# Attention and an ELU layer on one core: a path with constant scales, P V on array quarters, shared row sums, weight steps one by one

## The chip, the cores and the metric

The kernel runs on one core of a Trainium2 chip. The metric is the device time of one execution in microseconds (us). The kernel before took 647.91 us (median of 3 runs, 647.34 to 647.96). One more execution was run under the profiler; all rows below come from it. Of the core's engines, PE (TensorE) multiplies matrices, ACT (ScalarE) evaluates functions, DVE (VectorE) and POOL (GpSimd) work elementwise, and SP issues the DMAs.

## The reference

Attention over 48 heads (4 batches of 12 heads, 448 tokens, 64 columns a head), with scores bounded by a cap, and then two matrix products with an ELU between them. The cap is 30.

```
scale = 1.0 / np.sqrt(q.shape[-1])
scores = scale * np.matmul(q, k.transpose(0, 1, 3, 2))
scores = cap * np.tanh(scores / cap)
scores = scores - np.max(scores, axis=-1, keepdims=True)
attn = np.exp(scores)
attn = attn / (np.sum(attn, axis=-1, keepdims=True) + 1e-09)
attn_out = np.matmul(attn, v).astype(np.float32)
x = attn_out.transpose(0, 2, 1, 3).reshape(B * S, H * D)       # 1792 x 768
h = x @ w_in                                                    # 768 x 2048
g = np.where(h > 0.0, h, np.exp(np.minimum(h, 0.0)) - 1.0)
out = (g @ w_out).astype(np.float32)                            # 2048 x 768
```

## The kernel before

**Attention.** Two heads form a pair (24 pairs), and two pairs a round (12 rounds, `n`). Scores are kept with the keys on the partitions. The 448 keys of a head are cut into 64 + 3 x 128 (`NT` = 4 key tiles). A round has seven groups of scores: group 0 holds the first 64 keys of all four heads, stacked in one tile of two PSUM banks (`tile0`, plain f32); groups 1 to 3 and 4 to 6 hold the 128-key tiles of pair 0 and of pair 1 (`scores`, three products of f32 split in a high and a low part, `qkh` and `qkl`, which `prep_qk` makes on DVE). For each group ACT runs a tanh in place in PSUM and an exp into the SBUF tile `p` (`act`); the scale of each is a [128,1] tile that was worked out from the cap (`tsc`, `cap`).

**P V and row sums.** `values(n, i, t)` multiplies key tile `t` of pair `i` into the bank `pv` (tag `pv0`, one for both pairs of a round, one after the other): two matmuls, a head in each half of the array's columns. For `t` = 0 all 128 rows are used, with `v` zero in the rows of the other pair. `add` sums the three 128-key tiles of `p` in `u` on DVE, and `sums(n, i)` makes the row sums of a pair in the bank of tag `pv1`: ones times `u`, and a half-ones column times group 0, in four separate 32-row strips. `take` copies `pv` to `num` and the four strips to `sums` on DVE, and four small DMAs fold each pair's sums to 64 partitions; `invert` adds the two parts and eps, takes the reciprocal and sends it to DRAM; `spread` reads it back on all partitions, and `normalise` multiplies.

**PSUM.** The eight banks are three score tiles of two banks (tag `s`) and one bank each of `pv0` and `pv1`. A score group waits until the exp of the group three before it has read its tile.

**Order.** The order in the attention is written out by hand: `run` collects (time, function) events, sorts them and emits them; the times in `AT` are in units of one score group. Each engine runs its instructions in this order. Beside the attention DVE splits the tokens (`high`, `low`: xh, xl) and prepares the first four weights (`Weights.steps`, five steps a weight: three DVE operations; wq; DVE and POOL; wh; wl).

**The two products** (`Moe`). The tokens are cut in four blocks `t` of 512, 512, 512 and 256, the 2048 hidden columns in 8 rounds `r` of 256. A unit (r, t) has `first` (w_in, two tiles of 128 hidden columns into `pv0` and `pv1`, then `elu` over ACT, DVE, ACT, DVE) and `second` (w_out, six output tiles in three PSUM tiles of tag `s`, with e = 0, 2, 4). For r = 0 ACT copies the result to `acc`, later DVE adds it. PE's order is first(unit i), second(unit i-1). Around each `second` the weight steps of the next round are run: `n // 2` ahead of it and the rest behind it, `n` by block from `WRUN` = (6, 6, 4, 4). Here wq and wh are on ACT, and POOL's addition lies between them.

Which path runs is decided on the chip: every engine loads a flag (`|cap| <= 32`) and branches, to this path or to a general one.

Of the kernel before, what the change touches and what calls it, by code (L numbers as in the profile page):

```python
# [17 lines left out]
P = 128  # L18
# [13 lines left out]
FAST_CAP = 32.0  # L32
TINY = 2.0**-15
# [134 lines left out]
class Tokens:  # L168
# [17 lines left out]
    def high(self, p, t, vector=False):  # L186
# [12 lines left out]
        if vector:  # L199
            self.nc.vector.tensor_copy(out=out, in_=x)  # L200
        else:
            self.nc.scalar.activation(out=out, in_=x, func=AF.Copy)
# [11 lines left out]
class Moe:  # L214
# [57 lines left out]
    def second(self, r, t):  # L272
# [3 lines left out]
        for e in range(0, NC, 2):  # L276
# [46 lines left out]
class Attention:  # L323
# [51 lines left out]
    def tile0(self, n):  # L375
# [33 lines left out]

    def values(self, n, i, t):  # L410

        v = self.v[2 * n + i]
        if t == 0:
            x = [self.p[n, 0][:, j] for j in range(2)]
            self.pv[n, i] = self.ps.tile([P, BANK], F32, name=f"pv{n}_{i}", tag="pv0", bufs=1)
        else:
            pt = self.p[n, GROUP[i, t]]
            x = [pt[:, j] for j in range(2)]
        w = [v[:, t, j * D : j * D + D] for j in range(2)]
        self.two(self.pv[n, i], w, x, start=t == 0, stop=t == NT - 1)  # L420
# [11 lines left out]
    def sums(self, n, i):  # L432

        t = self.sum[n, i] = self.ps.tile([P, BANK], F32, name=f"sum{n}_{i}", tag="pv1", bufs=1)
        u = self.u.pop((n, i))
        work = [(self.ones, u[:, j]) for j in range(2)]
        work += [(self.half[:, i ^ j], self.p[n, 0][:, j]) for j in range(2)]
        for k, (w, x) in enumerate(work):
            self.nc.tensor.matmul(t[k * 32 : k * 32 + 32, :S], w, x, start=True, stop=True)  # L439

    def take(self, n, i, step):
        nc, sb, p = self.nc, self.sb, 2 * n + i
        if step == 0:
            t = self.num[p] = sb.tile([P, S], F32, name=f"num{p}", tag="num", bufs=5)
            nc.vector.tensor_copy(out=t, in_=self.pv.pop((n, i))[:, :S])  # L445
            return
        t = self.early.tile([P, S], F32, name=f"sums{p}", tag="ev", bufs=2)
        nc.vector.tensor_copy(out=t, in_=self.sum.pop((n, i))[:, :S])
        if i == 0:
            self.den[n] = sb.tile([CP, 2, 2, 2 * CN], F32, name=f"den{n}", tag="den", bufs=2)  # L450
        for k in range(4):
            j = slice(k % 2 * CN, k % 2 * CN + CN)
            nc.sync.dma_start(out=self.den[n][:, k // 2, i, j], in_=t[k * 32 : k * 32 + 1, :])

    def invert(self, n):

        nc = self.nc
        t = self.den.pop(n)
        den = t[:, 0]
# [5 lines left out]
        nc.sync.dma_start(  # L465
            out=d.rearrange("j (a n) -> a j n", a=CP), in_=den.rearrange("a i (j n) -> a (i j) n", j=2)
        )
# [14 lines left out]
    def run(self, weights, moe, raw, rawv):  # L482
# [14 lines left out]
        for n in range(rounds):  # L497
# [6 lines left out]
            for i in range(2):  # L504
                p = 2 * n + i
                for t in range(NT):
                    at(g + AT["values"][i][t], self.values, n, i, t)
                for step in range(2):
                    at(g + AT["add"][i][step], self.add, n, i, step)
                    at(g + AT["prep"][i][step], self.prep_qk, p + 2, step)  # L510
                    at(g + AT["take"][i][step], self.take, n, i, step)
                at(g + AT["sums"][i], self.sums, n, i)
# [3 lines left out]
                at(g + AT["load_v"][i], self.load_v, p + 2)  # L516
            at(min(g + AT["invert"], end + END["invert"]), self.invert, n)
# [3 lines left out]
            for k in range(2):  # L521
# [3 lines left out]
                for p in ([c] if 0 <= c < PPB else []) + [PPB + i for i in range(PPB) if n == 8 + i // 2]:  # L525
                    at(g + AT["split"][k], *((self.x.high, p, 0, True) if k == 0 else (self.x.low, p, 0)))
# [26 lines left out]
def general_attention(nc, sb, ps, x, con, src):  # L553
# [5 lines left out]
    for p in range(NPAIR):  # L559
# [3 lines left out]
        for j in range(2):  # L563
            o, o0 = slice(j * D, j * D + D), slice((p % 2 ^ j) * D, (p % 2 ^ j) * D + D)
# [34 lines left out]
def constants(nc, pool, cap):  # L599
# [3 lines left out]
    flag = pool.tile([1, 1], I32, name="flag")  # L603
# [4 lines left out]
    nc.vector.tensor_single_scalar(out=flag, in_=con.eps[0:1, :], scalar=FAST_CAP, op=ALU.is_le)  # L608
# [7 lines left out]
def attention_elu_kernel(tc, qk, v, cap, w, out):  # L616
    nc = tc.nc
    src = (qk, v)
    with ExitStack() as outer:
# [14 lines left out]
        fast = nc.values_load(flag[0:1, 0:1], min_val=0, max_val=1)  # L634

        def path(general):
            tag = "gf"[not general]
# [28 lines left out]
        with tc.If(fast > 0) as branch:  # L666
# [48 lines left out]
```

## Time and profile before

| | |
|---|---|
| median of 3 runs | 647.91 us |
| profiled execution | 648.52 us |
| its span | 646.7 us |
| PE busy | 629.4 us, 97% |
| DVE busy | 463.8 us, 72% |
| ACT busy | 296.7 us, 46% |
| POOL busy | 61.2 us, 9% |

The span is what the profile covers; 1.8 us of the execution lie around it. The attention fills the first 172 us, the rest is the two products. A share over the whole span says little here, since the stages have different limits; the rows below are therefore from short stretches. A granted clock (PEclk) of 1.00 is TensorE's higher level of 2.4 GHz.

### The profile page before, as it was taken

What the parts mean: (1) busy time and instruction counts of PE and PEld (TensorE: products, weight loads), DVE (VectorE), ACT (ScalarE), POOL (GpSimd) and SP (SyncE); (2) the same over time, 40 slices, a digit from 0 to 9 for tenths busy, and PEclk for the clock granted to TensorE, in tenths of its full rate; (3) what the DMA queues carried; (4) which work ended last, traced back from release to release, by engine and by line L of the source; (5) the groups of instructions that cost most, each with busy time, mean ns of one, the idle gap of its engine ahead of it and who ended that gap; (6) DMA issues with size and microseconds to landing.
All of it is one profiled execution on the core that took longest, in us unless ns stands there. A gap on an engine that the chain in (4) does not pass through costs nothing.

```text
span 646.7 us, 8796 instructions
## 1 busy us (share of the span) xinstructions
PE 629.4 (97%) x3408; PEld 463.0 (72%) x3408; DVE 463.8 (72%) x696; ACT 296.7 (46%) x396; POOL 61.2 (9%) x40
## 2 busy tenths in 40 slices
PE   5999999999999899999999999999999999999997
PEld 3334444334478788888888888888888888888886
DVE  4789999999667744776767577666857766776454
ACT  6999999999916544222231322223132322222110
POOL 0010100101001111121111111011111111211000
PEclk9999999999999999999999999999999999999999
DMA  4445565544123111121111111121111111200224
GB/s 162 140 141 186 158 185 148 168 125 132 32 77 126 51 49 50 49 98 31 68 50 50 49 50 55 43 76 71 50 50 50 50 50 49 70 30 0 98 97 152
DMA packets 30065, 54.38 MB, mean 84 GB/s; under 512 B 13377, under 2 KB 17473, under 8 KB 30017
## 3 DMA queue, kind: packets, MB, share of 16 engines
q1 hardware_dynamic: 30016, 53.75, 25.7%
q8 instruction: 29, 0.48, 0.3%
q14 instruction: 20, 0.16, 0.1%
HBM read 47.97 MB, written 5.59 MB: 83 GB/s over the span
## 4 chain that ended last, share of the span: by engine, by line
PE 78%; DVE 13%; DMA 3%; ACT 2%; issue 2%; POOL 1%; SPq 1%; DVEq 0%; POOLq 0%; ACTq 0%
PE o L226 11%; PE o L227 11%; PE o L228 11%; PE h L226 11%; PE h L227 11%; PE h L228 11%; PE pv L408 6%; PE s L366 4%; DVE u L430 3%; DVE xl L211 2%; PE sum L439 2%; DVE qkl L361 1%; DVE num L445 1%; PE s L383 1%; DMA den<-sums 1%
## 5 line engine op out<-in xcount | busy, mean ns | idle before, releaser
L226 PE MATMUL o<-gh,wh 128*128 128x512 f32 (+1 forms) x380 | 138.8, 365 | 2.7 <-ACT acc L285 2.7
L227 PE MATMUL o<-gl,wh 128*128 128x512 f32 (+1 forms) x380 | 138.9, 365 | 0.0
L228 PE MATMUL o<-gh,wl 128*128 128x512 f32 (+1 forms) x380 | 138.7, 365 | 0.0
L227 PE MATMUL h<-xl,wh 128*128 128x512 f32 x288 | 112.2, 390 | 0.3 <-DVE xl L211 0.3
L226 PE MATMUL h<-xh,wh 128*128 128x512 f32 x288 | 112.4, 390 | 0.0
L228 PE MATMUL h<-xh,wl 128*128 128x512 f32 x288 | 112.1, 389 | 0.0
L300 DVE TENSOR_TENSOR acc<-o,acc 128x1024 f32<-128x1024 f32 (+1 forms) x83 | 88.6, 1091 | 31.8 <-PE o L228 31.8
L240 ACT ACTIVATE e<-h 128x512 f32<-128x512 f32 (+1 forms) x64 | 34.7, 542 | 138.8 <-PE h L228 138.8
L401 ACT ACTIVATE p<-s,cap 128x896 f32<-128x896 f32 x84 | 84.7, 1008 | 2.7
L399 ACT ACTIVATE s<-s,tsc 128x896 f32<-128x896 f32 x84 | 81.9, 975 | 5.3 <-PE s L383 2.8
L226 PEld LDWEIGHTS o<-gh,wh 128*128 128x128 f32 x380 | 72.1, 190 | 14.5 <-ACT acc L285 2.9
L408 PE MATMUL pv<-p,vf 128*64 128x448 f32 x368 | 79.3, 552 | 3.0 <-DVE num L445 3.0
L228 PEld LDWEIGHTS o<-gh,wl 128*128 128x128 f32 x380 | 72.1, 190 | 11.4
L227 PEld LDWEIGHTS o<-gl,wh 128*128 128x128 f32 x380 | 72.0, 190 | 11.4
L249 ACT ACTIVATE gh<-e 128x512 fp32r<-128x512 f32 (+1 forms) x64 | 37.0, 578 | 90.2 <-DVE e L244 90.2
L250 DVE TENSOR_TENSOR gl<-e,gh 128x512 fp32r<-128x512 f32 (+1 forms) x64 | 40.0, 626 | 41.2 <-ACT gh L249 41.2
L142 POOL TENSOR_TENSOR pre<-pre,wq 128x768 int32<-128x768 int32 x18 | 34.7, 1929 | 339.7 <-DVE pre L139 339.7
L241 DVE TENSOR_SCALAR e<-e 128x512 f32<-128x512 f32 (+1 forms) x64 | 25.0, 391 | 56.5 <-ACT e L240 56.5
L226 PEld LDWEIGHTS h<-xh,wh 128*128 128x128 f32 x288 | 54.1, 188 | 12.4 <-DVE e L244 0.7
L227 PEld LDWEIGHTS h<-xl,wh 128*128 128x128 f32 x288 | 54.1, 188 | 11.6 <-DVE xl L211 0.7
L228 PEld LDWEIGHTS h<-xh,wl 128*128 128x128 f32 x288 | 54.1, 188 | 11.3
L408 PEld LDWEIGHTS pv<-p,vf 128*64 128x64 f32 x368 | 22.3, 136 | 44.1 <-issue 31.6
(78 smaller groups left out, 770.6 us busy)
## 6 DMA issues: line engine op xcount, KB each, us to landing
pre<-in_w_dram SPq DMA_DIRECT2D x18, 768.0 KB, 4.2
wr<-in_w_dram SPq DMA_DIRECT2D x14, 768.0 KB, 4.2
raw<-in_qk_dram SPq DMA_DIRECT2D x22, 448.0 KB, 4.5
vf<-in_v_dram SPq DMA_DIRECT2D x23, 256.0 KB, 4.1
rb<-rec SPq DMA_DIRECT2D x48, 112.0 KB, 2.9
out_dram<-acc SPq DMA_DIRECT2D x9, 512.0 KB, 2.7
den<-sums SPq DMA_DIRECT2D x96, 1.8 KB, 2.3
pre<-in_qk_dram SPq DMA_DIRECT2D x2, 256.0 KB, 4.1
```

The lines of the kernel that those rows point to most:

```text
L142: nc.gpsimd.tensor_tensor(out=vi, in0=vi, in1=q, op=ALU.add)
L226: mm(acc, wh[:, m, :], ph, start=first, stop=False)
L227: mm(acc, wh[:, m, :], pl, start=False, stop=False)
L228: mm(acc, wl[:, m, :], ph, start=False, stop=last)
L240: nc.scalar.activation(out=ev, in_=h, func=AF.Exp)
L249: nc.scalar.activation(out=gh, in_=ev, func=AF.Copy)
L250: nc.vector.tensor_tensor(out=gl, in0=ev, in1=gh.bitcast(F32), op=ALU.subtract)
L300: self.nc.vector.tensor_tensor(out=o, in0=s, in1=o, op=ALU.add)
L366: yield lambda a=a, b=b, i=i: self.nc.tensor.matmul(s, a[o, k], b[o, :S], start=i == 0, stop=i == 2)
L399: self.nc.scalar.activation(out=s, in_=s, func=AF.Tanh, scale=self.con.tsc[:, 0:1])
L401: self.nc.scalar.activation(out=pt, in_=s, func=AF.Exp, scale=self.con.cap[:, 0:1])
L408: self.nc.tensor.matmul(out[o, :S], w[j], x[j], **flags)
```

## The change

Six things change together.

- A third path, taken first when the cap is exactly 30: tanh and exp have their scales as constants in the instruction. A second flag is computed and loaded for it. The path otherwise equals the fast one.
- Group 0 is stacked by pair in all partitions (pair `i` in half `i`), and its P V uses quarters of the array: `values0` runs four matmuls of 64 rows x 64 columns, into two banks, one a pair. So `pv` has tag `pv0` for pair 0 and `pv1` for pair 1, and `sums` comes into `pv0` after pair 0's `num` has been taken.
- The row sums of both pairs are made in one bank, accumulated over `u` and group 0. One DVE instruction takes them and adds eps; four DMAs a round instead of eight; `invert` is a reciprocal alone.
- The high part of the tokens of block 0 (`high`) is made by ACT and no longer by DVE.
- The times in `AT` follow: both first tiles at 2.7, one `sums` at 8.25 and one `take_sums` at 8.9.
- `WRUN` gives the steps of a unit one place each: ahead of `second`, and behind each of its three output groups.

```
-WRUN = (6, 6, 4, 4)
+WRUN = ((2, 2, 1, 1), (2, 2, 1, 1), (2, 1, 1, 1), (1, 1, 1, 1))
 AT = {
-    "values": ((2.7, 2.8, 3.1, 4.7), (6.4, 6.5, 7.75, 7.8)),
+    "values0": 2.7, "values": ((2.8, 3.1, 4.7), (6.4, 6.5, 7.75)),
-    "sums": (6.2, 8.5), "take": ((5.35, 6.7), (8.75, 9.86)),
+    "sums": 8.25, "take": (5.35, 8.05), "take_sums": 8.9,
...
+            self.wt.run(steps[e // 2])            # in second, behind each e
...
-            n = WRUN[units[i - 1][1]]
-            self.wt.run(n // 2)
-            self.second(*units[i - 1])
-            self.wt.run(n - n // 2)
+            steps = WRUN[units[i - 1][1]]
+            self.wt.run(steps[0])
+            self.second(*units[i - 1], steps[1:])
...
-                o, at = slice(j * D, j * D + D), (i ^ j) * D            # tile0
+                o, at = slice(j * D, j * D + D), i * D
...
-        self.nc.scalar.activation(out=s, in_=s, func=AF.Tanh, scale=self.con.tsc[:, 0:1])
+        self.nc.scalar.activation(out=s, in_=s, func=AF.Tanh, scale=self.con.tanh_scale)
...
-        self.nc.scalar.activation(out=pt, in_=s, func=AF.Exp, scale=self.con.cap[:, 0:1])
+        self.nc.scalar.activation(out=pt, in_=s, func=AF.Exp, scale=self.con.exp_scale)
...
+    def values0(self, n):
+        for i in range(2):
+            o = slice(i * D, i * D + D)
+            pv = self.ps.tile([P, BANK], F32, name=f"pv{n}_{i}", tag=f"pv{i}", bufs=1)
+            self.pv[n, i] = pv
+            v = self.v[2 * n + i]
+            for j in range(2):
+                c = slice(j * D, j * D + D)
+                self.nc.tensor.matmul(
+                    pv[c, :S], v[o, 0, c], self.p[n, 0][o, j], start=True, stop=False
+                )
...
+    def sums(self, n):
+        t = self.sum[n] = self.ps.tile([P, BANK], F32, name=f"sum{n}", tag="pv0", bufs=1)
+        u = [self.u.pop((n, i)) for i in range(2)]
+        for last in range(2):
+            for k in range(4):
+                i, j = divmod(k, 2)
+                w, x = (self.half[:, i], self.p[n, 0][:, j]) if last else (self.ones, u[i][:, j])
+                self.nc.tensor.matmul(
+                    t[k * 32 : k * 32 + 32, :S], w, x, start=not last, stop=bool(last)
+                )
...
+    def take_sums(self, n):
+        nc, sb = self.nc, self.sb
+        t = self.early.tile([P, BANK], F32, name=f"sums{n}", tag="ev", bufs=2)[:, :S]
+        nc.vector.tensor_scalar_add(t, self.sum.pop(n)[:, :S], self.con.eps[:, 0:1])
+        self.den[n] = sb.tile([CP, 4, CN], F32, name=f"den{n}", tag="den", bufs=2)
+        for k in range(4):
+            nc.sync.dma_start(out=self.den[n][:, k, :], in_=t[k * 32 : k * 32 + 1, :])
...
-        nc.vector.scalar_tensor_tensor(
-            out=den, in0=den, scalar=self.con.eps[:CP, 0:1], in1=t[:, 1], op0=ALU.add, op1=ALU.add
-        )
...
+    nc.vector.tensor_single_scalar(out=flag[:, 1:2], in_=con.cap[0:1, :], scalar=USUAL_CAP, op=ALU.is_equal)
...
-        fast = nc.values_load(flag[0:1, 0:1], min_val=0, max_val=1)
+        fast, usual = (nc.values_load(flag[0:1, k : k + 1], min_val=0, max_val=1) for k in range(2))
+            if tag == "u":
+                con.tanh_scale, con.exp_scale = D**-0.5 / USUAL_CAP, USUAL_CAP
```

**PE, one round.** In a row's name the first number is the group, or the pair in `pv` and `sum`; the last is a running number of the buffer. Before, from the last product of pair 0 to pair 1's row sums (the six rows of the two score groups between are left out):

```order
L408 MATMUL pv_0_177<-p_3_183,pre 64x448 x2
L383 MATMUL s_0_217<-raw_126 64x448 x2
L383 MATMUL s_0_217<-raw_152 64x448 x2
L439 MATMUL sum_0_235<-u_0_185,ones 32x448 x2
L439 MATMUL sum_0_235<-p_0_147,half 32x448 x2
L408 MATMUL pv_1_240<-p_0_147,vf_115 64x448 x2
L408 MATMUL pv_1_240<-p_4_193,vf_115 64x448 x2
...
L408 MATMUL pv_1_240<-p_5_214,vf_115 64x448 x2
L408 MATMUL pv_1_240<-p_6_231,vf_115 64x448 x2
L439 MATMUL sum_1_277<-u_1_233,ones 32x448 x2
L439 MATMUL sum_1_277<-p_0_147,half 32x448 x2
```

And now, from `values0` on (score groups left out):

```order
L417 MATMUL pv_0_192<-p_0_162,pre 64x448 x2
L417 MATMUL pv_1_195<-p_0_162,vf_130 64x448 x2
L406 MATMUL pv_0_192<-p_1_165,pre 64x448 x2
...
L406 MATMUL pv_0_192<-p_3_201,pre 64x448 x2
L381 MATMUL s_0_235<-raw_141 64x448 x2
L381 MATMUL s_0_235<-raw_167 64x448 x2
L406 MATMUL pv_1_195<-p_4_211,vf_130 64x448 x2
L406 MATMUL pv_1_195<-p_5_232,vf_130 64x448 x2
...
L406 MATMUL pv_1_195<-p_6_249,vf_130 64x448 x2
L446 MATMUL sum_282<-u_0_203,ones 32x448 x2
L446 MATMUL sum_282<-u_1_251,ones 32x448 x2
L446 MATMUL sum_282<-p_0_162,half 32x448 x4
```

Pair 1's product with group 0 has moved from its own place behind `tile0` to pair 0's, and pair 0's row sums have moved behind pair 1's last product.

**ACT, the copies of unit (0, 1).** Before, from the end of the ELU of unit (0, 2):

```order
L249 ACTIVATE gh_2_2298<-e_2_2294 128x512
L135 ACTIVATE wq_2225<-wr_2076 128x768
L149 ACTIVATE wh_2305<-wv_2224 128x768
L285 ACTIVATE acc_0_2321<-o_1_0_2308 128x1024
L285 ACTIVATE acc_2_2336<-o_1_2_2323 128x1024
L285 ACTIVATE acc_4_2351<-o_1_4_2338 128x1024
```

And now:

```order
L247 ACTIVATE gh_2_2217<-e_2_2213 128x512
L136 ACTIVATE wq_2144<-wr_1995 128x768
L283 ACTIVATE acc_0_2237<-o_1_0_2224 128x1024
L150 ACTIVATE wh_2239<-wv_2143 128x768
L283 ACTIVATE acc_2_2256<-o_1_2_2243 128x1024
L283 ACTIVATE acc_4_2275<-o_1_4_2262 128x1024
```

The weight's high part, which waits for POOL, now stands behind the first copy and ahead of the other two.

**DVE, the additions of unit (6, 1).** Before:

```order
L139 SCALAR_TENSOR_TENSOR wv_4867<-wr_4758,wv_4867 128x768
L300 TENSOR_TENSOR acc_0_2321<-o_1_0_4933,acc_0_2321 128x1024
L300 TENSOR_TENSOR acc_2_2336<-o_1_2_4947,acc_2_2336 128x1024
L300 TENSOR_TENSOR acc_4_2351<-o_1_4_4961,acc_4_2351 128x1024
L153 TENSOR_TENSOR wl_4931<-wv_4867,wh_4930 128x768
```

And now:

```order
L140 SCALAR_TENSOR_TENSOR pre<-pre 128x768
L299 TENSOR_TENSOR acc_0_2237<-o_1_0_4865,acc_0_2237 128x1024
L154 TENSOR_TENSOR wl_4863<-pre,wh_4862 128x768
L124 SCALAR_TENSOR_TENSOR wv_4880<-wr_4804 128x768
L125 TENSOR_SCALAR wv_4880<-wv_4880 128x768
L126 TENSOR_SCALAR wv_4880<-wv_4880 128x768
L299 TENSOR_TENSOR acc_2_2256<-o_1_2_4885,acc_2_2256 128x1024
L299 TENSOR_TENSOR acc_4_2275<-o_1_4_4900,acc_4_2275 128x1024
```

Four weight operations have moved between the additions. The steps of a round r are now 21 and no longer 20, so the weights run ahead by one step a round; at this place the weight wh_4862 takes the buffer of a weight that PE still reads in first(6, 3), and its instruction waits for PE.

## Rows read from the trace of the kernel before

**Rows 1.** Two rounds: busy us of PE, PEld, DVE, ACT, POOL; PEclk; DMA share, GB/s.

```profile
45.40:59.00 13.60, 13.60 (x98) 5.66 (x97) 12.08 (x19) 13.37 (x15) 1.81 (x1) 1.00 0.61 192
141.60:156.00 14.40, 13.67 (x94) 5.59 (x92) 14.33 (x25) 13.44 (x15) 2.62 (x1) 1.00 0.51 151
```

**Rows 2.** Chain of waits in one round: start, us, what.

```profile
45.47 0.91 PE s L383 x8
46.38 0.89 PE sum L439 x8
47.27 1.65 PE pv L408 x8
48.92 1.41 PE s L366 x12
...
54.28 2.41 PE pv L408 x12
...
58.11 0.90 PE pv L408 x4
```

**Rows 3.** Timeline of ACT in a round: start, us, line, operation.

```profile
59.48 0.97 ACT L399 ACTIVATE s<-s,tsc 128x896 f32<-128x896 f32 x1
60.49 1.01 ACT L401 ACTIVATE p<-s,cap 128x896 f32<-128x896 f32 x1
61.39 0.97 ACT L399 ACTIVATE s<-s,tsc 128x896 f32<-128x896 f32 x1
```

**Rows 4.** Instructions by form: count, busy us, mean ns, idle before.

```profile
L401 ACT ACTIVATE p<-s,cap 128x896 f32<-128x896 f32 x84 | 84.7, 1008 | 2.7
L399 ACT ACTIVATE s<-s,tsc 128x896 f32<-128x896 f32 x84 | 81.9, 975 | 5.3 <-PE s L383 2.8 <-PE s L366 2.2
...
L285 ACT ACTIVATE acc<-o 128x1024 f32<-128x1024 f32 x9 | 8.5, 1022 | 0.0
...
L460 DVE SCALAR_TENSOR_TENSOR den<-den,eps 64x28 f32<-64x28 f32 x12 | 2.8, 233 | 0.0
...
L200 DVE CAST xh<-x 128x448 fp32r<-128x448 f32 x6 | 2.3, 378 | 0.0
...
L285 ACT ACTIVATE acc<-o 128x512 f32<-128x512 f32 x3 | 1.7, 598 | 0.0
```

**Rows 5.** Timeline of DVE: the copy of the sums and what follows.

```profile
54.23 0.62 DVE L448 COPY sums<-sum 128x448 f32<-128x448 f32 x1
54.76 1.08 DVE L430 TENSOR_TENSOR u<-p,p 128x896 f32<-128x896 f32 x1
```

**Rows 6.** Chain of waits at the start.

```profile
5.21 0.44 issue
5.65 2.09 PE s L383 x8
...
17.53 0.98 PE s L383 x8
```

**Rows 7.** Timeline of PE: last group 0, first product of the layer.

```profile
156.02 0.98 PE L383 MATMUL s<-raw 64*64 64x448 f32 x8
...
172.64 0.50 PE L226 MATMUL h<-xh,wh 128*128 128x512 f32 x1
```

**Rows 8.** Timeline of all engines from 218 us.

```profile
218.57 0.90 ACT L135 ACTIVATE wq<-wr 128x768 int32<-128x768 uint16 x1
...
222.33 0.84 ACT L149 ACTIVATE wh<-wv 128x768 fp32r<-128x768 f32 x1 [2.86 <-POOL wv L142]
223.08 2.83 ACT L285 ACTIVATE acc<-o 128x1024 f32<-128x1024 f32 x3
...
224.14 0.50 PE L226 MATMUL o<-gh,wh 128*128 128x512 f32 x1 [2.75 <-ACT acc L285]
```

**Rows 9.** Busy time by engine in the ten us around that wait.

```profile
220.00:230.00 10.00, 7.25 (x31) 5.86 (x30) 5.14 (x11) 5.78 (x9) 1.82 (x1) 0.83 0.25 80
```

**Rows 10.** Chain of waits: one product of the layer, 512 columns.

```profile
228.98 0.23 PE o L227
```

More of the change, by code (lines that the diff above doesn't have):

```diff
@@ L32 @@
 FAST_CAP = 32.0
+USUAL_CAP = 30.0
 TINY = 2.0**-15
@@ L198, in high @@
         out, x = self.parts[t, c][0][:, o : o + n], self.x[p][:, at : at + n]
[L199 to L202, printed above, removed]
+        self.nc.scalar.activation(out=out, in_=x, func=AF.Copy)
     def low(self, p, t):
@@ L270, in first, with second @@
                 self.elu(r, t, i, h)
-    def second(self, r, t):
+    def second(self, r, t, steps=()):
         nc = self.nc
@@ L408, in two @@
             self.nc.tensor.matmul(out[o, :S], w[j], x[j], **flags)
-    def values(self, n, i, t):
[L412 to L418, printed above, removed]
+    def values0(self, n):
[9 more added lines that the diff above has]
+                )
+    def values(self, n, i, t):
+        v, pt = self.v[2 * n + i], self.p[n, GROUP[i, t]]
+        x = [pt[:, j] for j in range(2)]
         w = [v[:, t, j * D : j * D + D] for j in range(2)]
-        self.two(self.pv[n, i], w, x, start=t == 0, stop=t == NT - 1)
+        self.two(self.pv[n, i], w, x, start=False, stop=t == NT - 1)
     def add(self, n, i, step):
@@ L430, in add @@
         self.nc.vector.tensor_tensor(out=self.u[n, i], in0=a, in1=b, op=ALU.add)
[L432 to L450, printed above, removed]
+    def sums(self, n):
[8 more added lines that the diff above has]
+                )
@@ new lines, in take @@
+    def take(self, n, i):
+        p = 2 * n + i
+        t = self.num[p] = self.sb.tile([P, S], F32, name=f"num{p}", tag="num", bufs=5)
+        self.nc.vector.tensor_copy(out=t, in_=self.pv.pop((n, i))[:, :S])
+    def take_sums(self, n):
[3 more added lines that the diff above has]
+        self.den[n] = sb.tile([CP, 4, CN], F32, name=f"den{n}", tag="den", bufs=2)
@@ L463, in invert @@
         nc.vector.reciprocal(out=den, in_=den)
         d = self.dr.tile([4, S], F32, name=f"rec{n}", tag="rec", bufs=2)
-        nc.sync.dma_start(
-            out=d.rearrange("j (a n) -> a j n", a=CP), in_=den.rearrange("a i (j n) -> a (i j) n", j=2)
-        )
+        nc.sync.dma_start(out=d.rearrange("k (a n) -> a k n", a=CP), in_=den)
         for i in range(2):
@@ L505, in run @@
                 p = 2 * n + i
-                for t in range(NT):
-                    at(g + AT["values"][i][t], self.values, n, i, t)
+                for t in range(1, NT):
+                    at(g + AT["values"][i][t - 1], self.values, n, i, t)
                 for step in range(2):
@@ L510, in run @@
                     at(g + AT["prep"][i][step], self.prep_qk, p + 2, step)
-                    at(g + AT["take"][i][step], self.take, n, i, step)
-                at(g + AT["sums"][i], self.sums, n, i)
+                at(g + AT["take"][i], self.take, n, i)
                 for f in ("spread", "normalise"):
@@ L516, in run @@
                 at(g + AT["load_v"][i], self.load_v, p + 2)
+            for f in ("values0", "sums", "take_sums"):
+                at(g + AT[f], getattr(self, f), n)
             at(min(g + AT["invert"], end + END["invert"]), self.invert, n)
@@ L602, in constants @@
         setattr(con, n, pool.tile([P, 1], F32, name=n))
-    flag = pool.tile([1, 1], I32, name="flag")
+    con.tanh_scale, con.exp_scale = con.tsc[:, 0:1], con.cap[:, 0:1]
+    flag = pool.tile([1, 2], I32, name="flag")
     nc.sync.dma_start(out=con.cap, in_=cap.broadcast_to([P, 1]))
@@ L607, in constants @@
     )
-    nc.vector.tensor_single_scalar(out=flag, in_=con.eps[0:1, :], scalar=FAST_CAP, op=ALU.is_le)
+    nc.vector.tensor_single_scalar(out=flag[:, 0:1], in_=con.eps[0:1, :], scalar=FAST_CAP, op=ALU.is_le)
+    nc.vector.tensor_single_scalar(out=flag[:, 1:2], in_=con.cap[0:1, :], scalar=USUAL_CAP, op=ALU.is_equal)
     nc.vector.reciprocal(out=con.tsc, in_=con.cap)
@@ L633, in attention_elu_kernel, with path @@
         nc.sync.dma_start(out=rawv0, in_=v[0])
[L634 to L637 removed]
+        fast, usual = (nc.values_load(flag[0:1, k : k + 1], min_val=0, max_val=1) for k in range(2))
+        def path(tag):
+            general = tag == "g"
+            if tag == "u":
+                con.tanh_scale, con.exp_scale = D**-0.5 / USUAL_CAP, USUAL_CAP
+            else:
+                con.tanh_scale, con.exp_scale = con.tsc[:, 0:1], con.cap[:, 0:1]
             with ExitStack() as ctx:
@@ L664, in path @@
                     moe.run()
-        with tc.If(fast > 0) as branch:
-            path(False)
+        with tc.If(usual > 0) as branch:
+            path("u")
         with branch.Else():
-            path(True)
+            with tc.If(fast > 0) as other:
+                path("f")
+            with other.Else():
+                path("g")
 def layouts(q, k, v, cap, moe_w_in, moe_w_out):
```

13 lines of the change are left out of this document (5 added, 8 removed).

## The prediction

> **What bounds the kernel now.** I read the busy time in stretches first, because the whole span mixes two stages. In a round of attention PE, ACT and DVE are all nearly full: in an early round PE 13.60 of 13.60 us, ACT 13.37, DVE 12.08; in a late one DVE 14.33 of 14.40, PE 13.67, ACT 13.44 [rows 1]. No one of them can be relieved alone. The chain of waits says who sets the end: in the round from 45.47 us it is PE without a gap, 0.91 + 0.89 + 1.65 + 1.41 + 1.65 + 0.89 + 1.41 + 2.41 + 1.42 + 0.90 = 13.54 us, where `tile0` is the 0.91, a pair's row sums 0.89, two steps of P V 1.65, three 2.41 and one alone 0.90, and two score groups 1.41 (the 1.65, 0.89 and 1.41 come two or three times, one row of each stands) [rows 2]. In late rounds DVE sets it, at 14.4. From the first `tile0` on the chain to the last one are 156.02 - 17.53 = 138.5 us for ten rounds, 13.85 each, and the last takes 172.64 - 156.02 = 16.6 [rows 6, 7]. In the two products PE is busy throughout, save at one place: PE waits 2.75 us for an ACT copy at 224.14 [rows 8], and the ten us around it have a mean granted clock of 0.83 [rows 9]. The engine was idle for those 2.75 us, and the clock then stood on the lower of its two levels, 1.2 GHz, for a while: 10 x (1 - 0.83) = 1.7 us of work lost beside the wait.
>
> **ACT.** Tanh to exp starts 1.01 us apart, exp to the next tanh 0.90, so a group costs 1.91 and a round 7 x 1.91 = 13.4 [rows 3]. What the scale tile costs is not to be seen alone. Copies from PSUM to SBUF without it take 1022 ns for 1024 columns and 598 for 512, so 916 for 896, where exp takes 1008 [rows 4]: 92 ns. For tanh, which writes to PSUM, there is no such row; its 975 bounds the gain between nothing and the same 92 (a loss is excluded, an operand is left out). I take 0.09 for each, since exp is the nearest row: 1.73 a group, 12.1 a round; with exp alone 12.75. The Trainium skill (ScalarE: Activation LUTs, What ACT_TABLE_LOAD costs) says that each [128,1] pointer operand adds about 93 ns to an ACTIVATE; by it tanh gains as much as exp. The trace agrees for exp (92 ns), and for tanh no run here shows it yet. ACT also gets the xh of block 0 in rounds 5 to 10: by the same copies some 0.5 us a round, and 0.3 more in rounds 8 to 10, so 12.6 to 12.9 there.
>
> **PE.** Two single steps of P V on the first keys go, and four quarter products come in one piece. No row shows quarter products into two `pv` banks, but `tile0` is four quarters too and takes 0.91 [rows 2]; if only two of the four overlapped, it would be two pairs one after the other, 1.65. I take 0.91. The two row sums stay 8 + 8 instructions, now behind one another, 1.78 at most. A round in the new order: 1.41 + 0.90 + 1.78 + 1.41 + 0.91 + 1.65 + 1.42 + 0.90 + 0.91 + 1.65 = 12.94 us, with the sums in one piece about 12.9: 0.64 less than before.
>
> **DVE.** One copy of sums goes, 54.76 - 54.23 = 0.53 [rows 5], and the addition of eps, 0.23 [rows 4], which the copy that stays takes along (I cost that at nothing; with a tile operand it may cost up to the 0.09 seen on ACT, once a round). The xh of rounds 5 to 10 goes too, 0.38 [rows 4], 0.3 without overlap, and two small ones in rounds 8 to 10, 0.2. A late round falls from 14.4 to 14.4 - 0.53 - 0.23 - 0.5 = 13.1; the others lie below PE's 12.9.
>
> **The rounds.** The longest of the three decides: eight rounds of 12.9 and the two late ones of 13.1 make 129.4. There is a new wait: `values0` writes the bank from which the row sums have just been taken. Between the sums and `values0` PE has two score groups, 1.41; DVE must by then have taken the sums, 0.62, behind `num` of pair 1 and xl. It has 0.8 us to spare if it is on time, and nothing in rounds with three weight operations more. Behind `values0` on PE stand the P V of pair 0 and groups 5 and 6, which ACT waits for. I allow 1.1 us for it in all: 130.5, a gain of 8.0. In the last stretch PE has 0.91 + 1.65 + 1.41 + 0.90 + 1.78 + 1.41 + 0.91 + 1.65 + 1.42 + 0.90 + 1.65 = 14.6 against 16.6, and behind the first product 0.90 + 1.78 against 1.65 + 0.89, 0.1 more: a gain of 1.9.
>
> **The start.** PE's first instruction comes 0.44 us behind the data [rows 6]; in that time the flag is loaded and the branch taken, and nothing hides a second flag. Its price lies between nothing and another 0.44; I take 0.2. The first `tile0` in the chain waits for five groups on ACT, 5 x 0.18 = 0.9 less. Net gain 0.7.
>
> **The stall at 221 us.** Before, the three copies stand behind wq and wh, and wh waits for POOL until 222.33 [rows 8]. Now the first copy stands ahead of wh: it can start where wh stood, behind wq at about 219.4, and ends at 220.4, before PE wants the bank at 224.14 - 2.75 = 221.4. The second copy stays behind wh, at 223.1 to 224.1; PE wants that bank one pair of outputs later, 12 products of 0.23 [rows 10] = 2.7, at 224.1. So the wait goes, with next to nothing to spare, and with it the lost clock: 2.75 + 1.7 = 4.4, of which I take 4.2. The Trainium skill (TensorE: Matmul & The Clock Gate, HAM oscillation — how this bites in real kernels) says that gaps in PE's work bring the clock down and that the loss is paid after the gap; the trace agrees, with the 0.83 behind the 2.75 us. What is late next is the third copy, which PE wants 2.7 us later still and which comes at 225.1.
>
> **A wait that is added.** In unit (6, 1) wl and three weight operations stand between the DVE additions, and wh waits for PE's last read of an old weight in first(6, 3), call it T. Then wh 0.85, wl 0.95, the three 2.0, the addition 1.2: T + 5.1. PE has the other half of first(6, 3), 2.05, and one output pair, 2.7, before it wants that bank: T + 4.8. Cost 0.3, once. Behind the waiting wh stand the ELUs of unit (6, 3), which have a whole `second` of time. Other units have one or two microseconds to spare.
>
> **Sum.** 8.0 + 1.9 + 0.7 + 4.2 - 0.3 = 14.5 us. The profiled execution took 648.5 (span 646.7, 1.8 around it), so 634.0; the median of the timed runs lies 0.6 below the profiled one, so I predict 633.4.
>
> **Rivals.**
> - *DVE still sets the rounds.* Heavy rounds, late sums and PE's wait at `values0` feed each other, as three engines with little slack did before, when rounds took 13.85 where PE's pieces make 13.54. With 13.3 a round the gain there is 5.5 less 1.1 for uneven rounds, about 4: 637.4. For it speaks DVE at 14.33 of 14.40; against it that its work falls more than PE's. Chance 15%.
> - *The stall moves.* The second copy comes later than reckoned, PE stops again and the clock falls again; 1 us stays of the 4.2: 636.6. The margin is under 0.1 us, but a short wait costs only itself. Chance 10%.
> - *The constants give ACT nothing.* Then ACT holds rounds at 13.4, and with xh 13.9 to 14.2: 137.7, a gain of 0.8 instead of 8.0; the start loses 0.2 and the last stretch gains about 0.4: 648.5 - 0.8 + 0.2 - 0.4 - 3.9 = 643.6, timed 643.0. Against it stands the 92 ns. Chance 4%.
> - *Quarters do not overlap in the new order.* `tile0` took one half and the other half of rows and columns in turn; now neighbours share columns, and in `values0` rows. At the program's start the same eight instructions took 2.09 us instead of 0.91 [rows 6]. At that price twice a round costs 2.36 more, 15.3 a round: 14 us lost in ten rounds, 0.5 in the last stretch; less 4.6 for the rest 658.4, timed 657.8: slower. It turns from faster to slower where a set of four costs about 1.5. Against it speaks that pairs that share rows (P V) and pairs that share columns (scores) overlap now. Chance 3%.
> - *The flag is not taken* (a cap that is not exactly 30 on the chip): the old scales in the new order, as the third rival. Within its chance.
>
> **How the numbers follow.** My forecast has 66%; its own range is 630.5 to 636, from tanh's bound, the flag and the waits. The range of 8 in 10 takes in the first two rivals and part of the third: 630 to 639.5. A change within 0.2% (1.3 us) can't be told from none. Faster: 66 + 15 + 10 + 4, less small change for what I have not thought of, 0.94; the quarters give slower 0.03, and 0.03 is left for the same.
>
> **What would show it.** Tanh and exp at about 885 and 915 ns and starts 1.73 apart where ACT has work; idle time on ACT in the rounds; a chain on PE with rounds of about 12.9; `tile0` and `values0` at 0.9 each; `den` in half as many DMAs; no wait of PE around 210 us and a clock of 1.00 in every stretch of the products. If rounds stay above 13.3 with waits of PE at `values0`, the DVE part is wrong; if exp stays at 1008, the ACT part; if PE waits for a copy again, the stall part.

## The result and the profile after

The changed kernel takes 637.71 us (median; 637.34 to 638.71, four runs), the kernel before beside it 647.93. The ratio is 0.9842, with a 95% interval of 0.9823 to 0.9861: faster by 10.2 us. 633.4 was predicted, within 630 to 639.5; the direction is right, a third of the gain is missing. The profiled execution took 637.5 us with a span of 635.7, against 648.5 and 646.7.

The span falls into five stretches, each cut at a row of the trace: to the second `tile0`, ten rounds, the last stretch of attention, the two products to DVE's last addition, and what follows that. After, PE's timeline has the cuts here (start, us, line, operation), as [rows 7] had them before:

```profile
16.66 0.98 PE L381 MATMUL s<-raw 64*64 64x448 f32 x8
...
149.41 0.98 PE L381 MATMUL s<-raw 64*64 64x448 f32 x8
...
163.73 0.50 PE L224 MATMUL h<-xh,wh 128*128 128x512 f32 x1
```

| Stretch | before, us | after, us | change | predicted |
|---|---|---|---|---|
| start to second `tile0` | 17.53 | 16.66 | -0.9 | -0.7 |
| ten rounds | 138.49 | 132.75 | -5.7 | -8.0 |
| last stretch | 16.62 | 14.32 | -2.3 | -1.9 |
| products, to DVE's last addition | 469.81 | 466.68 | -3.1 | -3.9 |
| behind the last addition | 4.25 | 5.29 | +1.0 | 0 |

The rounds are the largest miss. Their chain of waits is PE's alone in most of them (start, us, what). The second round, which has no wait, and single pieces of the third, the eighth and the ninth:

```profile
29.99 0.91 PE s L381 x8
30.90 1.65 PE pv L406 x8
32.55 1.41 PE s L364 x12
33.96 0.90 PE pv L406 x4
34.87 1.64 PE sum L446 x16
36.51 1.41 PE s L364 x9
37.92 0.92 PE pv L417 x8
38.83 1.65 PE pv L406 x8
40.49 1.42 PE s L364 x12
41.90 0.90 PE pv L406 x4
42.81 0.91 PE s L381 x8
...
47.69 2.49 PE sum L446 x16
...
117.15 1.51 PE pv L417 x8
...
128.77 0.61 DVE num L453
129.38 0.80 DVE xl L209 x3
130.18 0.61 DVE sums L458
130.79 0.04 issue
130.84 0.98 PE pv L417 x8
```

From 29.99 to 42.81 a round takes 12.82 us without a wait: `values0` 0.92, the sums in one piece 1.64, `tile0` 0.91. That is even 0.1 below the 12.9 predicted, so the quarters overlap as fully as [rows 2] let hope. Ten such rounds would take 128.2. The 4.55 us above that are PE's waits, and they show as pieces that grew: the sums from 1.64 to 2.49 in one round, `values0` from 0.92 to 1.51 in another; in the ninth the chain runs over DVE's `num`, `xl` and taken sums into `values0`. The 1.51 at 117.15 is a wait for V: the load of pair 1's V, issued at 111.26, lands at 117.66, and the first product that reads it starts at 117.70 (transfer, KB, us from issue to landing):

```profile
vf<-in_v_dram SPq DMA_DIRECT2D x1, 256.0 KB, 6.4
```

ACT did what was forecast of it, short of a little (line, operation, shapes, count | busy us, mean ns | idle before, against [rows 4]):

```profile
L399 ACT ACTIVATE p<-s 128x896 f32<-128x896 f32 x84 | 77.2, 919 | 2.7
L397 ACT ACTIVATE s<-s 128x896 f32<-128x896 f32 x84 | 76.5, 910 | 7.3 <-PE s L364 4.3 <-PE s L381 2.9
```

Exp lost 89 ns, tanh 65 of the 90 taken, and ACT now waits for PE 7.3 us in all. In the products PE waits twice, and shortly (the waits of PE after 185 us: total, times, longest), where [rows 8] had 2.75:

```profile
PE o L224 <- ACT acc L283: 0.4, 1, 0.4
PE o L224 <- DVE acc L299: 0.2, 1, 0.2
```

### The profile page after: what moved, and what is told of

Read it like the earlier page. It is cut to its first block, busy times and chain, and to the rows that moved or that the text cites. A ratio compares the mean times of both kernels' runs of the same rounds, so it can differ in the third digit from the quotient of the medians.

```text
span 635.7 us, 8710 instructions
## 1 busy us (share of the span) xinstructions
PE 622.6 (98%) x3408; PEld 459.9 (72%) x3408; DVE 456.6 (72%) x661; ACT 285.4 (45%) x408; POOL 61.2 (10%) x40
## 4 chain that ended last, share of the span: by engine, by line
PE 88%; DVE 5%; DMA 2%; ACT 2%; issue 1%; SPq 1%; POOL 1%; ACTq 0%; POOLq 0%; DVEq 0%
PE o L224 11%; PE o L226 11%; PE o L225 11%; PE h L224 11%; PE h L225 11%; PE h L226 11%; PE pv L406 9%; PE s L364 7%; PE sum L446 3%; PE pv L417 2%; PE s L381 2%; DVE xl L209 1%; DVE e L242 1%; DMA pre<-in_qk_dram 1%; DMA raw<-in_qk_dram 1%
## 5 line engine op out<-in xcount | busy, mean ns | idle before, releaser
L397 ACT ACTIVATE s<-s 128x896 f32<-128x896 f32 x84 | 76.5, 910 | 7.3 <-PE s L364 4.3
L399 ACT ACTIVATE p<-s 128x896 f32<-128x896 f32 x84 | 77.2, 919 | 2.7
L248 DVE TENSOR_TENSOR gl<-e,gh 128x512 fp32r<-128x512 f32 (+1 forms) x64 | 41.6, 651 | 41.3 <-ACT gh L247 41.3
L406 PE MATMUL pv<-p,vf 128*64 128x448 f32 x276 | 61.8, 556 | 0.0
L239 DVE TENSOR_SCALAR e<-e 128x512 f32<-128x512 f32 (+1 forms) x64 | 27.5, 430 | 45.4 <-ACT e L238 45.2
L242 DVE SCALAR_TENSOR_TENSOR e<-h,e 128x512 f32<-128x512 f32 (+1 forms) x64 | 40.0, 625 | 2.2
```

Of the source, the lines that this page charges most:

```text
L242: nc.vector.scalar_tensor_tensor(out=ev, in0=h, scalar=0.0, in1=ev, op0=ALU.max, op1=ALU.add)
L248: nc.vector.tensor_tensor(out=gl, in0=ev, in1=gh.bitcast(F32), op=ALU.subtract)
L406: self.nc.tensor.matmul(out[o, :S], w[j], x[j], **flags)
```

## Experiments

Theory A is the prediction's, made more exact by the trace after: the rounds are PE's pieces, 12.82, and PE's waits at the sums and at `values0` for DVE. The rivals: something else sets the remainder (ACT, or the transfers of q, k and V); the dealing had no part in the stall's going; the second flag and the nested branch cost what the end grew by. Each kernel was timed four to six times. They ran in four batches, each on one chip: rows 2 to 5 of the table; rows 1 and 6 to 8; rows 9 to 11; row 12. The kernel before, timed beside each, took 647.6 to 648.2 us. Their stretches, cut as above (us of one profiled execution each; the last column the median time and its range):

| Kernel | to 2nd tile0 | ten rounds | last stretch | products | end | time |
|---|---|---|---|---|---|---|
| changed, again | 16.67 | 134.41 | 14.33 | 467.04 | 4.85 | 638.79 (638.32-639.63) |
| pointer scales | 16.98 | 137.62 | 16.20 | 466.89 | 4.81 | 644.36 (643.91-646.37) |
| old dealing | 16.61 | 133.23 | 14.33 | 469.44 | 5.49 | 641.77 (639.56-644.38) |
| one flag | 17.84 | 134.62 | 14.32 | 466.61 | 5.51 | 640.24 (638.53-640.68) |
| no additions | 17.10 | 131.83 | 14.33 | 466.40 | 5.34 | 636.45 (635.58-637.90) |
| V before weights | 16.71 | 131.81 | 14.33 | 466.48 | 4.87 | 636.44 (636.01-636.73) |
| no additions, V first | 16.61 | 128.99 | 14.44 | 466.41 | 5.35 | 633.60 (633.22-633.92) |
| late sums | 19.23 | 129.21 | 12.54 | 467.73 | 5.39 | 635.90 (635.49-638.24) |
| late sums but first | 16.79 | 130.95 | 12.53 | 467.76 | 4.77 | 634.93 (634.43-635.70) |
| one flag, V first | 16.83 | 131.88 | 14.32 | 466.89 | 5.38 | 636.90 (635.77-638.11) |
| before without quarters | 17.89 | 136.10 | 16.11 | 466.28 | 4.02 | 640.56 (640.51-642.21) |
| even splits | 16.75 | 131.14 | 12.54 | 468.51 | 5.46 | 635.76 (635.31-636.36) |

**The scales as tiles again.**

```diff
-                con.tanh_scale, con.exp_scale = D**-0.5 / USUAL_CAP, USUAL_CAP
+                con.tanh_scale, con.exp_scale = con.tsc[:, 0:1], con.cap[:, 0:1]
```

> The changed kernel with the scales of tanh and exp read from [128,1] tiles again, as before; all else is left. Theory A (the constants are what frees ACT, and with them PE can set the rounds): a group costs ACT 0.89 + 0.065 more, 1.91 to 1.92 again, a round 13.4 and in rounds 5 to 10 13.9 with xh; the ten rounds go from 132.75 to 136 - 139, the start loses 0.8, the last stretch 0.5: 642 to 645 us. Theory B (PE's pieces and DVE set the rounds, the constants were worth little): ten rounds at 133 to 134, 638.5 to 639.5 us.

Measured 644.36 us, ratio to before 0.9953 (0.9936 to 0.9970). The ten rounds take 137.62, the last stretch 16.20. Two late rounds of this kernel by engine (window, us; busy us of PE, PEld, DVE, ACT, POOL; clock; DMA):

```profile
112.18:126.32 14.14, 13.85 (x92) 5.52 (x92) 12.10 (x18) 13.91 (x18) 1.82 (x1) 1.00 0.60 191
126.32:140.46 14.14, 13.80 (x92) 5.41 (x92) 13.70 (x22) 13.91 (x18) 0.00 (x0) 1.00 0.42 132
```

Three of its rounds are 14.14 long to the hundredth although DVE has 12.10 us of work in one and 13.70 in another: that is ACT above all, 13.91 busy (in the second the chain also runs over DVE's `num`, `xl` and sums). So A holds: without the constants the new order lets ACT set the late rounds, and 5.6 to 6.7 us of the gain hang on them, by the two medians of the changed kernel.

**The old dealing.**

```diff
-WRUN = ((2, 2, 1, 1), (2, 2, 1, 1), (2, 1, 1, 1), (1, 1, 1, 1))
+WRUN = ((3, 0, 0, 3), (3, 0, 0, 3), (2, 0, 0, 2), (2, 0, 0, 2))
```

> The changed kernel with weight steps dealt in two batches round second() again (3 and 3, 3 and 3, 2 and 2, 2 and 2). Theory A (the order of wh and the first copy is what removed the stall): PE waits some 2.7 us for an ACT copy again at about 213 us, the clock falls behind it, and the stretch from the first product to the last addition grows from 466.7 to about 469.8; the wait in unit (6, 1) goes: 641 us. Theory B (the stall went because fewer weight steps or other data were late): 637.7 us, no wait.

641.77 us; the products take 469.44 in place of 466.68. PE's waits there, and the ten us around (columns as above):

```profile
PE o L224 <- ACT acc L283: 3.6, 1, 3.6
```

```profile
210.00:220.00 10.00, 6.35 (x42) 5.61 (x41) 5.48 (x9) 6.09 (x8) 1.80 (x1) 1.00 0.23 80
```

The stall is back at the forecast place, and the wait in unit (6, 1) is gone, so A holds. One thing differs from before: the wait is longer, 3.6 against 2.75, and the granted clock stays at 1.00, the upper level, where [rows 9] have 0.83. That is this execution's, not the program's: of the six timed executions three have a mean granted clock of 0.999 to 1.000 over the whole run and take 639.56 to 640.97 us, three have 0.993 to 0.995 and take 642.57 to 644.38. So one and the same program keeps its clock in some executions and loses part of it in others, and the two sets lie 3.1 us apart in the mean; where in the run it is lost the timed executions do not say.

**One flag, two paths.** The `usual` flag alone chooses between the path with constants and the general one; the flag `fast`, its path and the nested branch go:

```diff
-            with tc.If(fast > 0) as other:
-                path("f")
-            with other.Else():
-                path("g")
+            path("g")
```

> The changed kernel with one flag and two paths: the constants' path where cap is 30, else the general one. Theory A (the second flag costs 0.2 us at the start and the nested branch nothing at the end): first product issued 0.2 us earlier, end as before, 637.5 us. Theory B (the nested branch also costs the 1.0 us by which the end after the last addition grew, 5.29 against 4.25): 636.4 us, with 4.2 to 4.3 us behind the last addition.

640.24 us, slower than the changed kernel, against both theories. The end behind the last addition is 5.51 without a nested branch, so that is not what lengthened it. Its profiled span is 3.2 us longer, 1.2 at the start, where its chain runs over the second half of q and k and its first score products come every 0.37 us a pair up to 12.0 us (in the changed kernel every 0.20 from 9.0 us on; the trace's record of the granted clock begins at 13.45 us here, at 8.94 there, so what it was before is not recorded), and 1.9 in the rounds: two rounds with a weight load took 14.87 and 13.77, where the changed kernel has 13.68 and 13.12. Its rounds hold the same instructions, which raised the question whether transfers differ between executions.

**Without the additions of P tiles.** The row sums take the third tile alone:

```diff
-        self.nc.vector.tensor_tensor(out=self.u[n, i], in0=a, in1=b, op=ALU.add)
+        self.u[n, i] = p[2]
```

> The changed kernel without the additions of P tiles on DVE: the row sums take the third tile alone, so 4 additions of about 1.0 us a round go from DVE, and the output is not the reference's. Theory A (what the ten rounds take beyond PE's pieces, 132.75 against 128.2, is PE's wait for DVE at the sums and at values0): rounds of 12.8 to 12.9, ten of them 128.5, span 631.5, time 633.3. Theory B (ACT or the loads of raw and v set the rest): rounds stay at 13.1 or more, 636 or more.

636.45 us: some 4 us of DVE work a round went, and the time fell by 1.3 us only. But the ten rounds say more than their sum: 13.44, 12.82, 14.02, 12.82, 12.83, 13.47, 12.83, 13.96, 12.81, 12.83. Six are PE's 12.82, so far A. The other four are rounds 1, 3, 6 and 8, those with a weight load. Its chain names the reason (start, us, what), and SP's queue shows what stood ahead (start, us, line, transfer, count):

```profile
44.34 0.93 PE pv L406 x4
45.27 0.34 SPq L543
45.61 0.05 issue
45.66 6.80 DMA vf<-in_v_dram
52.47 0.04 issue
52.51 0.97 PE pv L417 x4
```

```profile
43.74 0.93 SPq L106 DMA_DIRECT2D pre<-in_w_dram  x1
44.76 0.85 SPq L543 DMA_DIRECT2D raw<-in_qk_dram  x2
45.66 0.62 SPq L549 DMA_DIRECT2D vf<-in_v_dram  x1
```

V of the second pair lands 6.8 us after its issue, behind 768 KB of weights and twice 448 KB of q and k, and `values0` (L417) waits for it. Each theory was half right. Before, the second pair's V was wanted at place 6.4 of its round; `values0` wants both at 2.7.

**The changed kernel again.** No edit.

> The changed kernel, unaltered, beside the runs that follow, to see how far start, rounds and end move from one program execution and chip to the next. Theory A (one flag lost 2.5 us by other means than the flag): 637.5 to 638 us, the ten rounds at 132.7 +- 0.3, the end behind the last addition at 5.3. Theory B (the DMAs of a start and of the rounds with a weight load differ that much between executions): 637.5 to 640, the ten rounds between 132.7 and 134.6.

638.79 us; ten rounds of 134.41, with 14.75 in round 3. The same program thus differs by 1.7 us in its rounds, and the chain shows V there too:

```profile
45.22 7.89 DMA vf<-in_v_dram
53.12 0.04 issue
53.16 0.97 PE pv L417 x4
```

Theory B: executions, or the chips they ran on, differ, and the one-flag kernel's rounds, 134.62, lie beside these.

**V before the weights.** The weight load is issued behind the loads of q, k and V of its round:

```diff
-    "weights": (4.95, 5.68), "wload": -2.0, ...
+    "weights": (4.95, 5.68), "wload": -1.55, ...
```

> The changed kernel with the weight load issued behind the loads of q, k and V of its round, not ahead of them (one number). Theory A (values0 asks for V of both pairs at once, and in the four rounds with a weight load V of the second pair lands too late behind 768 KB): values0 takes 0.92 in every round but the two of the chain through DVE, the ten rounds lose 0.7 to 1.5: 636.2 to 637.0 us. Theory B (V was no bound in the changed kernel, DVE hides it): no change, 637.7.

636.44 us (636.01 to 636.73), below every run of the changed kernel. No wait for V is left; the ten rounds take 131.81, with 12.82 in round 1 and 13.25 in round 3. So A: one number was worth 1.3 to 2.4 us. What is left, 131.81 - 128.2 = 3.6, are waits at the sums, in rounds 3, 4, 5, 8 and 10, and at `values0` in round 9, behind DVE's taken sums.

**Both together.** No additions and V first, to see whether anything else remains.

> Without the additions of P tiles, as in the experiment of that name (the output is not the reference's), and with the weight load behind the loads of q, k and V. There six rounds took 12.82 and the four with a weight load 13.44, 14.02, 13.47 and 13.96. Theory A (those four wait for V): ten rounds of 12.82 to 12.85, 128.3, 3.5 us less: 633.0 us. Theory B (the weight transfer itself holds something else up, wherever it is issued): 13.4 to 14.0 stay in those rounds, 636.

633.60 us, so A in the main. Nine of the ten rounds take 12.82 to 12.85; the fourth takes 13.52, with 0.7 us of wait at `values0`. That is V once more: the load for the second pair, issued at 57.37 behind twice 448 KB of q and k and with no weights ahead of it, lands at 63.72, and the product that reads it starts at 63.77 (transfer, KB, us from issue to landing):

```profile
vf<-in_v_dram SPq DMA_DIRECT2D x1, 256.0 KB, 6.3
```

The ten rounds take 128.99. The remainder of the rounds is therefore DVE's lateness (131.81 - 128.99 = 2.8) and V's; ACT has no share in it.

**The sums later.** With V first, PE's order gives DVE more time: the sums one score burst (two score groups) later, all P V of a pair behind one burst; in the last round `END` holds the sums where they were:

```diff
-    "values0": 2.7, "values": ((2.8, 3.1, 4.7), (6.4, 6.5, 7.75)),
-    "sums": 8.25, "take": (5.35, 8.05), "take_sums": 8.9,
+    "values0": 4.06, "values": ((4.07, 4.08, 4.7), (7.6, 7.65, 7.75)),
+    "sums": 9.06, "take": (5.35, 8.05), "take_sums": 9.3,
...
```

> The changed kernel with the weight load behind V, and on PE the row sums one score burst later, values0 and the P V of the first pair one burst later, the P V of the second pair one burst later too; the last round's sums stay where they are. Theory A (PE waits at the sums for DVE's last addition, at values0 for the taken sums and for V): in rounds 1 to 7 a chain on PE with 12.82 to 12.9, in the three rounds with three more subtractions 13.2 to 13.9; ten rounds 129.5 to 131.5, 634.5 to 637 us. Theory B (DVE or ACT is the bound whatever the order): no gain, 637.7, or worse where ACT runs dry in the longer stretch without scores.

635.90 us, within A's range. The rounds fall to 129.21: 12.54, 12.53, 12.65, 12.88, 12.87, 12.89, 12.90, 13.17, 13.22, 13.56. From one round's chain:

```profile
34.17 2.41 PE pv L406 x12
...
37.99 1.65 PE sum L446 x16
...
41.05 0.91 PE pv L417 x8
41.96 2.41 PE pv L406 x12
```

The P V of a pair now runs as one piece of 2.41 where it was 1.65 + 0.90, so even PE's sum is shorter, 12.5. But 2.5 us are lost ahead of the second `tile0` (0.6 of them the first data) and 1.3 in the products, into which P V of the last round has moved; the last stretch gives 1.8 back.

**Late sums, but not in the first round.**

```diff
+                late = AT[f] if n or f != "values0" else 2.7
-                at(min(g + AT[f], end + END.get(f, 99)), getattr(self, f), n)
+                at(min(g + late, end + END.get(f, 99)), getattr(self, f), n)
...
```

The first pair's P V of the first round keeps its old places too (2.8, 3.1, 4.7).

> The order with late sums, but in the first round, where PE waits for ACT's first groups anyway, values0 and the P V of the first pair stay at their old places. Theory A (what the late order lost at the start, 19.23 against 16.71 us to the second tile0, of which 0.6 is the landing of the first data, is work put behind the bursts): the second tile0 at 17 to 17.5 us, ten rounds still 129.2 to 129.6: 634.0 us. Theory B (the start is ACT's and the later order only shows it): second tile0 still near 18.6, 635.6 us.

634.93 us, ratio to before 0.9805 (0.9789 to 0.9821); the changed kernel's intervals are 0.9823 to 0.9861 and 0.9829 to 0.9881. This version beats both kernels. Where the microsecond came from is less clear: the second `tile0` came at 16.79, but the round behind it took 14.27 in place of 12.54, so that the third `tile0` came at 31.06 against 31.77, and 0.5 of that is the landing of the first data. ACT's first groups set the start, as theory B has it: the chain runs over ACT's groups up to 19.84 us. The time came out between the two theories, and the place of the second `tile0` alone was no good measure of the start.

**One flag again, with V first.** The edit of one flag on the kernel with V first.

> One flag and two paths, with the weight load behind V, so that the rounds are the same as in the run with two flags and V first (636.4). Theory A (the second flag costs 0.2 at the start and nothing else): 636.2 us, end behind the last addition 4.8 to 5.5. Theory B (flag and nested branch cost 1.2): 635.2 us. Theory C (the one-flag program is slower by itself, as its 640.2 looked): 638.5 us or more.

636.90 us against 636.44: no difference that can be told. The start of both chains, with two flags (first) and with one:

```profile
4.79 0.56 issue
5.36 1.91 PE s L381 x8
```

```profile
4.85 0.18 issue
5.03 2.36 PE s L381 x8
```

The second flag delays PE's first instruction by 0.38 us, near the upper bound given. Yet the products of group 0 (x8) then take 2.36 in place of 1.91 and the first tanh starts at 7.47 against 7.35: they read four loads of q and k, and the last of these lands at 6.72 against 6.46, later than the flag. In this pair the flag costs nothing that can be told. Of the 640.24 of the first one-flag run the 1.9 us in the rounds lie within what two executions of the changed kernel differ by; its 1.2 us at the start came again in the kernel before without quarters, which has one flag too (17.89), and not here (16.83), so whether one flag has a part in them stays open.

**The kernel before, without quarters and joint sums.** Before, with constants (behind its one flag), dealing and xh on ACT.

> The kernel before with all parts of the change but one: constants (behind its one flag), xh on ACT, weight steps dealt singly; P V of the first keys and the row sums stay pair by pair. Theory A (PE's pieces are the bound, so quarters and the joint sums are worth their 0.64 us a round and DVE's 0.76): PE's 13.54 in most rounds, 14.0 to 14.3 in a few, ten rounds 136.5 to 138, last stretch 16.0, stall gone: 641.5 to 643 us. Theory B (constants, xh and dealing carry the gain): 638 us.

640.56 us, ten rounds of 136.10, both a little below A's ranges. Its rounds are 13.54 or 13.55 in seven of ten cases, the PE sum of [rows 2], so there PE's pieces bind; the 14.3 to 14.5 that three rounds of before took are gone with the constants and xh on ACT. Quarters and joint sums brought 1.8 to 2.9 us of time as they stand, and 4.1 with V first. These differences also hold a start that is 1.2 us longer here and an end that is 0.8 to 1.3 shorter; in the rounds and the last stretch alone it is 3.5 to 5.1 as they stand.

**Splits spread.**

```diff
-    "split_from": 5, ... if n == 8 + i // 2
+    "split_from": 4, ... enumerate((7, 8, 9, 9, 10, 10)) if n == k
```

> The late order of the run before, with the splits of block 0 spread: large ones in rounds 4 to 9 in place of 5 to 10, the six small ones in rounds 7, 8, 9, 9, 10, 10 in place of 8, 8, 9, 9, 10, 10. Theory A (in rounds 8 to 10 DVE is late for values0 by its three subtractions): those rounds fall from 13.2, 13.2 and 13.6 to 13.0 to 13.2, round 4 grows by 0.2: 634.3 us. Theory B (ACT sets these rounds and only the work's sum counts): 634.9, no change.

635.76 us, no better: rounds 5 and 7 grow by 0.2 and 0.1, round 8 falls by 0.1, round 10 stays at 13.57. A fails; ACT's part in these rounds is only moved about, as B has it. The products are 0.8 longer, 0.7 of it a wait for an ACT copy that the run before did not have.

## Why the prediction came out as it did

- **PE's pieces: right.** 12.82 measured, 12.9 forecast.
- **The waits of the rounds: the step that failed.** "I allow 1.1 us for it in all" and 13.1 for two late rounds made 130.5. PE's waits were 4.55 us, and more in another execution. Two things were missed. First, V: the working asked only when the bank of the sums is free, not when the other inputs of `values0` arrive. The P V of the second pair's first keys moved forward by 3.7 of 7 places, past the margin that its load had; the experiment with V first shows 0.9 to 2.6 us for that, and in one round of the run without additions V is late even with no weights ahead of it. Second, DVE's average was taken for its punctuality. Below PE's 12.9 in sum, it is late in the rounds in which a weight step holds it up, since the joint sums need the last addition of both pairs at once. POOL's four additions of the attention begin at 43.41, 71.27, 109.36 and 137.73, in rounds 3, 5, 8 and 10, and in each of these the sums take longer than 1.64: 2.49, 2.07, 2.00 and 1.75. With V first, leaving out DVE's additions took 2.8 us off the ten rounds. Two such places in the changed kernel, DVE's timeline (start, us, line, operation, idle before) and POOL's beside both:

```profile
45.25 0.56 DVE L152 CAST wh<-pre 128x768 fp32r<-128x768 f32 x1 [1.54 <-POOL pre L143]
...
47.34 1.09 DVE L436 TENSOR_TENSOR u<-u,p 128x896 f32<-128x896 f32 x1 [0.53 <-DVE u L436]
...
71.10 1.09 DVE L436 TENSOR_TENSOR u<-p,p 128x896 f32<-128x896 f32 x1
72.29 2.55 DVE L436 TENSOR_TENSOR u<-u,p 128x896 f32<-128x896 f32 x1
```

```profile
43.41 1.81 POOL L143 TENSOR_TENSOR pre<-pre,wq 128x768 int32<-128x768 int32 x1 [37.70 <-DMA rb<-rec]
71.27 2.63 POOL L143 TENSOR_TENSOR pre<-pre,wq 128x768 int32<-128x768 int32 x1 [26.05 <-DVE pre L140]
```

  The sums at 47.69 take 2.49 behind the first, those at 74.52 2.07 behind the second.
- **Last stretch: right**, -2.3 for -1.9. The forecast added it up from PE's pieces alone, but it needs the constants as much: with pointer scales it takes 16.20, without the quarters 16.11, of 16.62 before.
- **Start: right in size, in good part by luck.** Of the -0.9, 0.5 is the first load of q and k, which landed at 4.70 in place of 5.21. The flag cost its 0.2 (PE's first product 0.63 behind the data for 0.44). The constants were to give 0.9 and gave less: from PE's first product to the second `tile0` are 11.33 us after 11.88, and with pointer scales 11.64. Tanh gave 65 ns, not 90, and the chain is ACT's only up to 10.93 us; from there on it is PE's.
- **The stall: right in place, cause and size.** The wait for the copy fell from 2.75 to 0.4 and the lost clock of 1.7 went: 4.1 of the 4.2. The wait added in unit (6, 1) came as 0.2 for 0.3 (its four terms make T + 5.0, not T + 5.1). Still the products fell by 3.1, not 3.9: PE waits 0.5 us and not 0.3 at their first units, and the sums behind the first product cost 0.1, which the forecast had put to the last stretch; for the other 0.3 no single wait shows. The lost clock is the least sure term: the timed executions of before have mean clocks of 0.994 to 0.999, and the old dealing keeps it in some and not in others.
- **The end: not forecast.** 1.0 us more behind the last addition. All programs with the quarters have 4.8 to 5.5 there, with one flag or two; the two without have 4.25 and 4.02. In that stretch the instruction queue has four packets in the former and three in the latter (queue, packets, MB, share; the changed kernel first, then before):

```profile
q14 instruction: 4, 0.03, 2.4%
```

```profile
q14 instruction: 3, 0.02, 1.9%
```

  That goes with it in all fourteen profiles; that it is the cause was not tried.
- **Rivals.** The constants and the quarters did what was hoped, and the flag was taken: three rivals fell clearly. The 2.09 us that priced the quarters' rival was no price of overlap: at the start the four loads that those products read land from 5.21 to 6.85 us, and the products run from 5.65 to 7.74. The stall did not move either: a wait of 0.4, with the clock at 1.00 behind it. "DVE still sets the rounds" is the one whose time, 637.4, came out. Its mechanism was half the truth: DVE's lateness was there, V's beside it.

## What to carry over

When work is moved forward, follow every operand it reads to its transfer, and look at what stands ahead of that transfer in its queue; the bank it writes is only one of its conditions. An engine whose work per round is below the bound can still be late: look where the joined instruction needs its last result, in the worst round and not in the mean. And cut the result at rows into stretches before explaining it: here two executions of one program differ by 1.7 us in the rounds, more than several of the edits.

## What was not expected of the hardware

- An addition on DVE that takes 1.09 us took 2.55 beside a POOL operation of 2.63 that began 1.0 us earlier (above); the POOL operation itself takes 1.81 where no DVE addition runs, and here began inside an earlier addition, of 71.10 to 72.19. At 137.73 the same comes again, 2.61 and 2.54. The Trainium skill (SBUF — State Buffer, SBUF: two separate sides) says that DVE and GpSimd share one pair of ports as an exclusive lock, which the one that comes first keeps for its whole instruction; the trace agrees: 71.27 + 2.63 = 73.90 and another 0.94 to 74.84, the end of the addition, and POOL's 0.82 of excess ends at 72.09, where the earlier addition does within 0.1.
- A PE wait of 2.75 us was followed by a clock of 0.83 in its ten us [rows 9], one of 3.6 us at the same place by 1.00. The clock fell in some executions of one program and not in others (the old dealing); what decides between them these runs do not show.
- P V in three steps without a change of operation between them took 2.41 us, the same twelve instructions in two pieces 1.65 + 0.90 = 2.55.
- V's transfers of 256 KB, in two executions of the changed kernel: those for the first pair, with no large load issued just ahead, took 2.6 to 3.1 us from issue to landing; those for the second pair, behind 2 x 448 KB of q and k, 4.1 to 6.0, and with 768 KB of weights ahead of these 6.3 to 7.9.
